# Mixture-of-experts block after a sketched attention: second expert product by seven half-width products on 2x2 blocks, token weights multiplied into x

## The chip, the cores and the metric

The kernel runs on one core of a Trainium2 chip. The metric is the device time of one execution in microseconds. A core has a matrix engine (PE, TensorE), a vector engine (DVE), a scalar engine (ACT), a general engine (POOL, GpSimd) and an engine that issues transfers (SP). Each engine works through its own list of instructions in order and waits on semaphores for the others. PE reads its operands from SBUF and writes to PSUM, which has eight banks of 512 float32 columns on 128 partitions.

## What is computed

The input of the second block is the output of the first, so both are in the kernel. All of it is float32.

```python
# attention: batch 4, heads 4, sequence 1088, head_dim 32, r = 8
def phi(x):                                   # 64 products of two sketches
    a = np.einsum('rd,bhsd->bhsr', S1, x)
    b = np.einsum('rd,bhsd->bhsr', S2, x)
    return np.einsum('bhsi,bhsj->bhsij', a, b).reshape(*x.shape[:-1], r * r)
q_p, k_p = (phi(q), phi(k))
kv = np.einsum('bhsf,bhsd->bhfd', k_p, v)
z = np.sum(k_p, axis=2)
num = np.einsum('bhsf,bhfd->bhsd', q_p, kv)
den = np.einsum('bhsf,bhf->bhs', q_p, z)[..., None] + 1e-06
x = num / den                                 # as 4352 tokens x 128
# routing and experts: N = 4352 tokens, D = 128, E = 8 experts, F = 1024
P = np.exp(x @ w_gate - (x @ w_gate).max())
for _ in range(8):
    P /= P.sum(1, keepdims=True) + 1e-09
    P /= P.sum(0, keepdims=True) + 1e-09
    P *= N / E
for e in range(E):
    h = np.maximum(x @ w1[e], 0.0)
    out += P[:, e:e + 1] * (h @ w2[e])
```

P is positive. A product with it may therefore stand in front of the maximum with zero as well as behind the second product.

## The kernel before

**Attention** (lines 184 to 255) runs four times, once for a batch of 1088 tokens. A pass transposes k and q on DVE (L187 to L191), projects k on PE (L197, L201), copies that to SBUF on ACT (L199, L202), forms the 64 products of the keys on DVE (L207), and sums them with v on PE (L214). DVE masks the sums (L221, L222). Then three chunks of 384, 352 and 352 tokens follow. A chunk projects q by four matmuls on two halves of PE's rows (L235), copies two of the four results on ACT (L238), multiplies them with the other two on DVE (L239), and forms denominators and numerators by four matmuls on two halves of PE's columns (L244). DVE adds a constant, takes a reciprocal and multiplies (L247 to L249), which gives the chunk's columns of `xT`, that is x with its 128 features on partitions. At the end of a pass come the logits: matmuls of 128 tokens each with `w_gate` as the moving operand of 8 columns (L254).

**Routing** (lines 263 to 298) is a chain on DVE with one small matmul on PE in each of its eight rounds (L285), for the sums over tokens. At its end the weights are spread over partitions (L296, L298).

**Experts** (lines 344 to 358): outside the 8 experts, inside 9 tiles of 512 tokens (the last has 256). A tile takes 8 blocks of 128 hidden units; each is one matmul of the first product (L351), a maximum with zero on ACT (L353), and one matmul of the second product one block later (L340), which accumulates in PSUM. DVE transposes the sum of a tile and expert in blocks of 32 (L324), multiplies it with the tokens' weights (L331) and adds it to `acc` (L332). The last expert's tiles are stored by SP (L311).

**What sets the order.** The kernel is written in the order attention, routing, experts, for a scheduler that sorts the instructions of each engine by the order in which they are written and by when their operands and buffers are to be had. The attention and the routing take their PSUM from a pool of four banks (`aps`, through `bank()`), the first product from a pool of two (`hps`), the second from another of two (`yps`). In the built program matmuls of expert 0 stand between those of the attention from the second pass on, and two pairs of them between each two rounds of the routing. The weights of expert 0 are loaded at the start from POOL's queue, the other experts' from the same queue, and k, q and v from SP's.

A matmul of float32 shows in the trace as two records, each with a weight load of its own.

Of the kernel before, what the change touches and what calls it, by code (L numbers as in the profile page):

```python
# [18 lines left out]
def f64_to_f32(nc, pool, raw, shape):  # L19
    """Pairs of 32-bit words (low, high) of float64 to float32, rounded to nearest: the upper 24 bits  # L20
    of the mantissa are a float32 by themselves, and the 29 bits below are added to it."""
# [15 lines left out]
    # The power of two, with its sign.  # L37
# [8 lines left out]
    # Below float32's normal range: zero; above it: infinite.  # L46
# [8 lines left out]
def kernel(  # L55
# [26 lines left out]
    UP = 2.0 ** 64  # L82

    consts = ctx.enter_context(tc.tile_pool(name="consts", bufs=1))
    big = ctx.enter_context(tc.tile_pool(name="big", bufs=1))
    ld = ctx.enter_context(tc.tile_pool(name="ld", bufs=2))
    wk = ctx.enter_context(tc.tile_pool(name="wk", bufs=2))
    wpool = ctx.enter_context(tc.tile_pool(name="wpool", bufs=3))
    hpool = ctx.enter_context(tc.tile_pool(name="hpool", bufs=4))
    ypool = ctx.enter_context(tc.tile_pool(name="ypool", bufs=3))  # L90
    sk = ctx.enter_context(tc.tile_pool(name="sk", bufs=2))
    hps = ctx.enter_context(tc.tile_pool(name="hps", bufs=2, space=PSUM))
    yps = ctx.enter_context(tc.tile_pool(name="yps", bufs=2, space=PSUM))
    aps = ctx.enter_context(tc.tile_pool(name="aps", bufs=4, space=PSUM))

    def bank():
        return aps.tile([P, 512], F32, tag="a", name="a")

# [8 lines left out]
    for i in range(2):  # L107
        t = consts.tile([P, H + 1, NT + 1, D], F32, name=f"v{i}")
        nc.gpsimd.memset(t[:, 2], 1.0)
        v_slots.append(t)  # L110
# [23 lines left out]
    weights = {}  # L134

    def load_w(e):
        w1 = wpool.tile([P, F], F32, tag="w1", name="w1")
        w2 = wpool.tile([P, FO, DM], F32, tag="w2", name="w2")
        nc.gpsimd.dma_start(out=w1, in_=moe_w1[e])  # L139
        nc.gpsimd.dma_start(out=w2, in_=moe_w2[e].rearrange("(fo fi) d -> fi fo d", fi=P))  # L140
        weights[e] = w1, w2
# [3 lines left out]
    load_w(0)  # L145

# [9 lines left out]
    rep = consts.tile([P, 4, 32], F32, name="rep")  # L156
    for c in range(4):
        sl = slice(32 * c, 32 * (c + 1))
        nc.gpsimd.tensor_copy(rep[sl], ident[sl, sl].unsqueeze(1).to_broadcast([32, 4, 32]))

    # The projections: wd gives a head's a and b, wq gives them repeated to the 64 products of a head.
# [15 lines left out]
    # Columns of x: (b, a, s).  # L177
    xT = big.tile([P, N], F32, name="xT")
    lg = big.tile([P, NG, E], F32, name="lg")
    acc = big.tile([P, NB, 32], F32, name="acc")  # L180
    prep = big.tile([P, NG, 4, E], F32, name="prep")

# [1 line left out]
    def attention(b):  # L184
# [8 lines left out]
        # Keys: a and b with tokens on partitions, their products, and the sums with v and 1.  # L193
# [22 lines left out]
        # Two heads together: the blocks of a head with the other's are zero.  # L216
# [10 lines left out]
        # Queries: the products with tokens in columns, then numerators and denominators.  # L227
# [22 lines left out]

        g0, g1 = b * S // P, (b + 1) * S // P
        pg = bank()[:, 0:(g1 - g0) * E].rearrange("p (g e) -> p g e", e=E)
        for g in range(g0, g1):
            nc.tensor.matmul(pg[:, g - g0, :], xT[:, P * g:P * (g + 1)], wg, start=True, stop=True)  # L254
        nc.scalar.copy(lg[:, g0:g1, :], pg)

    for b in range(B):
        attention(b)
        if b + 1 < 3:
            load_w(b + 1)  # L260

# [1 line left out]
    def routing():  # L263
        mx = sk.tile([P, 1], F32, tag="mx", name="mx")
        nc.vector.tensor_reduce(out=mx, in_=lg, axis=AX.XY, op=Alu.max)
        pm = bank()[:, 0:P]
        nc.tensor.matmul(pm, mx.to_broadcast([P, P]), ident, start=True, stop=True)
        nc.vector.reduce_max(mx, pm, axis=AX.X)
        nc.vector.tensor_scalar(mx, mx, -1.0, 64 * math.log(2.0), op0=Alu.mult, op1=Alu.add)
        pw = sk.tile([P, NG, E], F32, tag="p2", name="p2")  # L270
        nc.scalar.activation(out=pw, in_=lg, func=Act.Exp, bias=mx[:, 0:1])
        # float32's smallest step, 2^-149, which the exponentials are multiples of.
        step = 1.5 * 2.0 ** (23 - 149 + 64)
        nc.vector.tensor_scalar(pw, pw, step, step, op0=Alu.add, op1=Alu.subtract)
        for _ in range(ITERS):
            rs = sk.tile([P, NG], F32, tag="rs", name="rs")
            nc.vector.reduce_sum(rs, pw, axis=AX.X)
            nc.vector.tensor_scalar(rs, rs, 1.0 / UP, 1e-9, op0=Alu.mult, op1=Alu.add)
            nc.vector.reciprocal(rs, rs)
            p1 = sk.tile([P, NG, E], F32, tag="p1", name="p1")  # L280
            nc.vector.tensor_tensor(p1, pw, rs.unsqueeze(2).to_broadcast([P, NG, E]), op=Alu.mult)
            cs = sk.tile([P, E], F32, tag="cs", name="cs")
            nc.vector.reduce_sum(cs, p1.rearrange("p g e -> p e g"), axis=AX.X)
            pc = bank()[:, 0:E]
            nc.tensor.matmul(pc, ones, cs, start=True, stop=True)  # L285
            cr = sk.tile([P, E], F32, tag="cr", name="cr")
            nc.vector.tensor_scalar(cr, pc, 1.0 / UP, 1e-9, op0=Alu.mult, op1=Alu.add)
            nc.vector.reciprocal(cr, cr)
            pw = sk.tile([P, NG, E], F32, tag="p2", name="p2")
            nc.vector.scalar_tensor_tensor(pw, p1, float(N) / E, cr.unsqueeze(1).to_broadcast([P, NG, E]),  # L290
                                           op0=Alu.mult, op1=Alu.mult)
        # From partitions (c, s) to (any of four, s), as the outputs' blocks have them.
        for c in range(4):
            sl = slice(32 * c, 32 * (c + 1))
            pp = bank()[:, 0:NG * E]
            nc.tensor.matmul(pp, rep[sl].rearrange("p r s -> p (r s)"), pw[sl].rearrange("p g e -> p (g e)"),  # L296
                             start=True, stop=True, tile_position=(32 * c, 0))
            nc.scalar.mul(prep[:, :, c, :], pp.rearrange("p (g e) -> p g e", e=E), 1.0 / UP)  # L298

    routing()  # L300
    pcols = prep.rearrange("p g c e -> p (g c) e")

# [1 line left out]
    tiles = [(lo, min(lo + 512, N)) for lo in range(0, N, 512)]  # L304

    def store(b0, b1):
        while b0 < b1:
            b, a = divmod(b0, SA)
            m = min(b1 - b0, SA - a)
            for r in range(4):  # L310
# [3 lines left out]
                    in_=acc[32 * r:32 * (r + 1), b0:b0 + m, :])  # L314
            b0 += m

    def combine(e, lo, hi, yp):
        b0, b1 = lo // 32, hi // 32
        part = acc[:, b0:b1, :]
        if e == 0:  # L320
            nc.vector.transpose(out=part.rearrange("p b d -> p (b d)"), in_=yp)  # L321
            return
        yt = ypool.tile([P, 16, 32], F32, tag="yt", name="yt")[:, 0:b1 - b0, :]
        nc.vector.transpose(out=yt.rearrange("p b d -> p (b d)"), in_=yp)  # L324

        def weight(i):
            return pcols[:, b0:b1, i].unsqueeze(2).to_broadcast([P, b1 - b0, 32])

        if e == 1:
            nc.vector.tensor_tensor(part, part, weight(0), op=Alu.mult)  # L330
        nc.vector.tensor_tensor(yt, yt, weight(e), op=Alu.mult)  # L331
        nc.vector.tensor_tensor(part, part, yt, op=Alu.add)  # L332
        if e == E - 1:
            store(b0, b1)

    waiting = []

    def second():
        e, lo, hi, fo, hT, yp = waiting.pop(0)
        nc.tensor.matmul(yp, weights[e][1][:, fo, :], hT, start=(fo == 0), stop=(fo == FO - 1))  # L340
        if fo == FO - 1:
            combine(e, lo, hi, yp)

    for e in range(E):
        if e not in weights:
            load_w(e)
        for lo, hi in tiles:
            yp = yps.tile([P, 512], F32, tag="y", name="y")[:, 0:hi - lo]
            for fo in range(FO):
                hp = hps.tile([P, 512], F32, tag="h", name="h")[:, 0:hi - lo]  # L350
                nc.tensor.matmul(hp, weights[e][0][:, P * fo:P * (fo + 1)], xT[:, lo:hi], start=True, stop=True)  # L351
                hT = hpool.tile([P, 512], F32, tag="hT", name="hT")[:, 0:hi - lo]
                nc.scalar.activation(out=hT, in_=hp, func=Act.Relu)  # L353
                waiting.append((e, lo, hi, fo, hT, yp))
                if len(waiting) > 1:
                    second()
    while waiting:
        second()
# [30 lines left out]
```

## Time and profile before

| what | us |
|---|---|
| median of 3 runs | 1061.43 |
| lowest, highest | 1061.02, 1062.99 |
| span of the profiled execution, first to last instruction | 1058.4 |
| PE busy in that span | 1032.3 |
| ACT busy, DVE busy, POOL busy | 347.7, 240.8, 14.8 |
| L351 and L340, busy | 562.5 and 561.5 |
| last `xT` of the four attention passes written | 54.6, 83.3, 110.9, 135.9 |
| routing, from its first DVE instruction to its last on ACT | 138.7 to 174.9 |
| last matmul's start, end of the span | 1052.4, 1058.4 |

The profiled execution's span is 3.0 us shorter than the median of the runs, which count what lies around the span too. Busy times of matmuls overlap, since one's end is drawn behind the next one's start; what a matmul costs is read from the distance between starts. In the profile's clock row, and in the clock column of its tables, the first record is at 38.2 us; a full clock shown ahead of that is not a reading.

### The profile page before, as it was taken

What the parts mean: (1) busy time and instruction counts of PE and PEld (TensorE: products, weight loads), DVE (VectorE), ACT (ScalarE), POOL (GpSimd) and SP (SyncE); (2) the same over time, 40 slices, a digit from 0 to 9 for tenths busy, and PEclk for the clock granted to TensorE, in tenths of its full rate; (3) what the DMA queues carried; (4) which work ended last, traced back from release to release, by engine and by line L of the source; (5) the groups of instructions that cost most, each with busy time, mean ns of one, the idle gap of its engine ahead of it and who ended that gap; (6) DMA issues with size and microseconds to landing.
All of it is one profiled execution on the core that took longest, in us unless ns stands there. A gap on an engine that the chain in (4) does not pass through costs nothing.

```text
span 1058.4 us, 7579 instructions
## 1 busy us (share of the span) xinstructions
PE 1032.3 (98%) x2806; PEld 499.9 (47%) x2806; DVE 240.8 (23%) x405; ACT 347.7 (33%) x618; POOL 14.8 (1%) x34
## 2 busy tenths in 40 slices
PE   3999999999999999999999999999999999999997
PEld 3555544454444544454445444454445444454444
DVE  3665565111111211111111111111111111121112
ACT  0122223333333333333333333333333333333332
POOL 2000000000000000000000000000000000000000
PEclk9999999999999999999999999999999999999999
DMA  7200000000000100010000100010000000001111
GB/s 267 85 22 1 1 1 0 1 21 20 0 1 0 40 0 1 0 41 0 1 0 1 40 1 0 1 40 1 1 0 1 0 1 0 1 0 21 20 20 25
DMA packets 25683, 17.78 MB, mean 17 GB/s; under 512 B 20528, under 2 KB 22576, under 8 KB 25648
## 3 DMA queue, kind: packets, MB, share of 16 engines
q1 hardware_dynamic: 23168, 8.92, 3.2%
q0 software_dynamic: 2304, 8.39, 2.5%
q8 instruction: 22, 0.36, 0.1%
q14 instruction: 13, 0.11, 0.0%
q10 hardware_dynamic: 176, 0.01, 0.0%
HBM read 15.08 MB, written 2.23 MB: 16 GB/s over the span
## 4 chain that ended last, share of the span: by engine, by line
PE 96%; DMA 1%; DVE 1%; issue 0%; SPq 0%; ACT 0%; DVEq 0%; ACTq 0%
PE h L351 44%; PE y L340 44%; PE a L235 2%; PE a L244 2%; PE a L214 2%; DMA kx<-in_k_dram 1%; PE a L254 1%; DMA v<-in_v_dram 1%; PE a L197 1%; DVE kT L187 0%; DVE qa L239 0%; PE a L285 0%; SPq L123 0%; DVE kp L207 0%; PE a L201 0%
## 5 line engine op out<-in xcount | busy, mean ns | idle before, releaser
L351 PE MATMUL h<-xT,w 128*128 128x512 f32 (+1 forms) x1152 | 562.5, 570 | 0.0
L340 PE MATMUL y<-hT,w 128*128 128x512 f32 (+1 forms) x1152 | 561.5, 569 | 0.1
L353 ACT ACTIVATE hT<-h 128x512 f32<-128x512 f32 (+1 forms) x576 | 330.2, 573 | 610.5 <-PE h L351 610.5
L340 PEld LDWEIGHTS y<-hT,w 128*128 128x128 f32 x1152 | 217.4, 190 | 248.1 <-issue 236.5
L351 PEld LDWEIGHTS h<-xT,w 128*128 128x128 f32 x1152 | 217.5, 190 | 243.5 <-issue 240.1
L324 DVE STREAM_TRANSPOSE yt<-y 128x512 f32<-128x512 f32 (+1 forms) x63 | 43.3, 687 | 686.4 <-PE y L340 686.4
L331 DVE TENSOR_TENSOR yt<-yt,prep 128x512 f32<-128x512 f32 (+1 forms) x63 | 41.7, 662 | 2.1
L332 DVE TENSOR_TENSOR acc<-acc,yt 128x512 f32<-128x512 f32 (+1 forms) x63 | 41.7, 662 | 2.1
L238 ACT COPY qa<-a 128x352 f32<-128x352 f32 (+1 forms) x24 | 11.1, 461 | 61.9 <-PE a L235 61.9
L214 PE MATMUL a<-v,kp 128*128 128x96 f32 x144 | 23.9, 321 | 6.9 <-DVE kp L207 6.9
L235 PE MATMUL a<-qT,wq 64*128 64x352 f32 (+1 forms) x96 | 29.8, 546 | 0.0
L248 DVE RECIPROCAL rd<-rd 128x352 f32<-128x352 f32 (+1 forms) x12 | 29.0, 2416 | 0.4
L214 PEld LDWEIGHTS a<-v,kp 128*128 128x128 f32 x144 | 21.5, 225 | 11.0 <-DVE kp L207 7.0
L235 PEld LDWEIGHTS a<-qT,wq 64*128 64x128 f32 x96 | 14.4, 208 | 12.2 <-issue 6.1
L197 PE MATMUL a<-wd,kT 128*128 128x64 f32 x64 | 9.6, 313 | 10.8 <-DVE wd L171 10.8
L244 PE MATMUL a<-qa,kz 128*64 128x352 f32 (+1 forms) x48 | 15.8, 544 | 2.7 <-DVE qa L239 2.7
L321 DVE STREAM_TRANSPOSE acc<-y 128x512 f32<-128x512 f32 (+1 forms) x9 | 6.1, 679 | 53.7 <-PE y L340 53.7
L244 PE MATMUL a<-qa,kv 128*64 128x352 f32 (+1 forms) x48 | 15.5, 526 | 0.0
L197 PEld LDWEIGHTS a<-wd,kT 128*128 128x128 f32 x64 | 9.1, 227 | 10.7 <-issue 10.7
L139 POOL DMA_DIRECT2D w<-in_moe_w_dram x8 | 4.6, 578 | 682.6 <-PE h L351 682.6
L239 DVE TENSOR_TENSOR qa<-qa,a 128x352 f32<-128x352 f32 (+1 forms) x24 | 12.0, 509 | 5.2 <-PE a L235 4.9
L207 DVE TENSOR_TENSOR kp<-ab 128x1024 f32<-128x1024 f32 (+1 forms) x12 | 10.9, 946 | 3.8 <-ACT ab L199 3.8
(73 smaller groups left out, 118.2 us busy)
## 6 DMA issues: line engine op xcount, KB each, us to landing
w<-in_moe_w_dram POOLq DMA_DIRECT2D x16, 512.0 KB, 4.9
kx<-in_k_dram SPq DMA_DIRECT2D x4, 544.0 KB, 4.3
qx<-in_q_dram SPq DMA_DIRECT2D x4, 544.0 KB, 3.3
v<-in_v_dram SPq DMA_DIRECT2D x32, 64.0 KB, 2.0
out_dram<-acc SPq DMA_DIRECT2D x20, 64.0 KB, 1.9
v<-in_v_dram SPq DMA_DIRECT2D x16, 8.0 KB, 3.0
out_dram<-acc SPq DMA_DIRECT2D x4, 56.0 KB, 1.8
out_dram<-acc SPq DMA_DIRECT2D x4, 48.0 KB, 1.8
```

Source lines behind the costliest of these rows:

```text
L197: nc.tensor.matmul(pk[:, t].rearrange("p n f -> p (n f)"), kT[:, P * t:P * (t + 1)], wdf, start=True, stop=True)
L214: nc.tensor.matmul(pv[:, i], kp[0:n, g:g + 2].rearrange("p h i j -> p (h i j)"), vx[0:n, 2 * i:2 * i + 3, t, :], start=(t == 0), stop=(t = ...
L235: nc.tensor.matmul(t[:, 0:n], wqf[sl, m, :], qT[sl, lo:hi], start=True, stop=True, tile_position=(64 * i, 0))
L239: nc.vector.tensor_tensor(qa[:, 0:n], qa[:, 0:n], pb[:, 0:n], op=Alu.mult)
L244: nc.tensor.matmul(t[64 * i:64 * (i + 1), 0:n], w[:, i].rearrange("p h d -> p (h d)"), ph[i][:, 0:n], start=True, stop=True, tile_position ...
L248: nc.vector.reciprocal(rd[:, 0:n], rd[:, 0:n])
L324: nc.vector.transpose(out=yt.rearrange("p b d -> p (b d)"), in_=yp)
L331: nc.vector.tensor_tensor(yt, yt, weight(e), op=Alu.mult)
L332: nc.vector.tensor_tensor(part, part, yt, op=Alu.add)
L340: nc.tensor.matmul(yp, weights[e][1][:, fo, :], hT, start=(fo == 0), stop=(fo == FO - 1))
L351: nc.tensor.matmul(hp, weights[e][0][:, P * fo:P * (fo + 1)], xT[:, lo:hi], start=True, stop=True)
L353: nc.scalar.activation(out=hT, in_=hp, func=Act.Relu)
```

## The change

The second product is done on 2x2 blocks. Two tiles of tokens (t = 0, 1) and two neighbouring blocks of hidden units (f = 0, 1) make the four blocks h0 to h3; `w2` is split into two halves of 64 output columns. Where the plain way takes eight products of 64 output columns, seven are formed here, from sums of blocks: the sums of `w2` come from POOL (`ws`, four additions for each load of an expert), the sums of h from DVE (`ts`, four subtractions for each four blocks of h). The seven go to four accumulators in PSUM, and their sums are taken apart once for each group (`evacuate`).

Both products are now made of matmuls of 64 output columns, which stand alternately on the left and on the right half of PE's columns (`tile_position` 0 and 64). The built program has 1,280 of them in the first product and 1,120 in the second.

The loops are exchanged: outside 5 pairs of token tiles (three of 2x448, two of 2x416), inside the experts. A step of four h blocks and seven products is a quad; there are 160. Expert 0 goes first over three pairs without weights, and is weighted when it is added; elsewhere the weights multiply x on POOL (`xe`), from a copy of P that goes through DRAM (`pT`) and back to all partitions (`pb`). Each expert is loaded anew for each pair, by SP.

The logits are made at the end of each chunk, with `w_gate` (8 columns) as the weights and the chunk's `xT` as the moving operand, and land transposed (`lgT`). The first product uses the pool `aps` (through `bank()`) that attention and routing use; `hps` and `yps` are gone, and four banks hold the accumulators.

In the built program PE's list is: attention passes 1 to 4, in each of them the chunk's logits ahead of the next chunk's L235; then all nine matmuls of the routing; then the experts. No matmul of an expert stands ahead of the routing's last.

Cut to its core:

```diff
-    hps = ctx.enter_context(tc.tile_pool(name="hps", bufs=2, space=PSUM))
-    yps = ctx.enter_context(tc.tile_pool(name="yps", bufs=2, space=PSUM))
     aps = ctx.enter_context(tc.tile_pool(name="aps", bufs=4, space=PSUM))
+    mps = ctx.enter_context(tc.tile_pool(name="mps", bufs=1, space=PSUM))
+    dram = ctx.enter_context(tc.tile_pool(name="dram", bufs=1, space=bass.MemoryType.DRAM))
...
+    def load_w(e, queue):
         w1 = wpool.tile([P, F], F32, tag="w1", name="w1")
         w2 = wpool.tile([P, FO, DM], F32, tag="w2", name="w2")
-        nc.gpsimd.dma_start(out=w1, in_=moe_w1[e])
-        nc.gpsimd.dma_start(out=w2, in_=moe_w2[e].rearrange("(fo fi) d -> fi fo d", fi=P))
-        weights[e] = w1, w2
+        queue.dma_start(out=w1, in_=moe_w1[e])
+        queue.dma_start(out=w2, in_=moe_w2[e].rearrange("(fo fi) d -> fi fo d", fi=P))
+        ws = wpool.tile([P, 4, FO // 2, H2], F32, tag="ws", name="ws")
+        a11, a21 = w2[:, 0::2, 0:H2], w2[:, 0::2, H2:DM]
+        a12, a22 = w2[:, 1::2, 0:H2], w2[:, 1::2, H2:DM]
+        nc.gpsimd.tensor_tensor(ws[:, 0], a21, a22, op=Alu.add)
+        nc.gpsimd.tensor_tensor(ws[:, 1], ws[:, 0], a11, op=Alu.subtract)
+        nc.gpsimd.tensor_tensor(ws[:, 2], a11, a21, op=Alu.subtract)
+        nc.gpsimd.tensor_tensor(ws[:, 3], a12, ws[:, 1], op=Alu.subtract)
+        return w1, w2, ws
...
-        g0, g1 = b * S // P, (b + 1) * S // P
-        pg = bank()[:, 0:(g1 - g0) * E].rearrange("p (g e) -> p g e", e=E)
-        for g in range(g0, g1):
-            nc.tensor.matmul(pg[:, g - g0, :], xT[:, P * g:P * (g + 1)], wg, start=True, stop=True)
-        nc.scalar.copy(lg[:, g0:g1, :], pg)
+            pg = bank()[32 * b:32 * b + E, 0:n]
+            nc.tensor.matmul(pg, wg, xT[:, b * S + lo:b * S + hi], start=True, stop=True,
+                             tile_position=(0, 32 * b))
+            nc.scalar.copy(lgT[32 * b:32 * b + E].rearrange("p a s -> p (a s)")[:, lo:hi], pg)
...
+        nc.vector.transpose(out=lgp.rearrange("p a e -> p (a e)"), in_=lgT.rearrange("p a s -> p (a s)"))
+        lg = lgp[:, :, 0:E]
...
+        nc.vector.transpose(out=lgT.rearrange("p a s -> p (a s)"), in_=lgp.rearrange("p a e -> p (a e)"))
+        for b in range(B):
+            nc.sync.dma_start(out=pT[:, b * S:(b + 1) * S],
+                              in_=lgT[32 * b:32 * b + E].rearrange("p a s -> p (a s)"))
...
+    groups = [(i, [0], False) for i in range(PLAIN)]
+    groups += [(i, list(range(1 if i < PLAIN else 0, E)), True) for i in range(NP)]
+    items = [(g, e) for g, (_, es, _) in enumerate(groups) for e in es]
...
+        pb = late.tile([P, 2 * NMAX], F32, tag="pb", name="pb")[:, 0:2 * n]
+        nc.sync.dma_start(out=pb, in_=pT[e:e + 1, lo:lo + 2 * n].to_broadcast([P, 2 * n]))
+        xe = late.tile([P, 2 * NMAX], F32, tag="xe", name="xe")[:, 0:2 * n]
+        nc.gpsimd.tensor_tensor(xe, xT[:, lo:lo + 2 * n], pb, op=Alu.mult)
+        sources[j] = xe
...
+    def evacuate(g):
+        i, _, weighted = groups[g]
+        lo, n = pair(i)
+        m = []
+        for k in range(4):
+            t = late.tile([P, NMAX], F32, tag=f"m{k}", name="m", bufs=1)[:, 0:n]
+            if k % 2:
+                nc.vector.tensor_copy(t, sums[g][k])
+            else:
+                nc.scalar.copy(t, sums[g][k])
+            m.append(t)
...
+    def first(k, c):
+        j, q = quads[k]
+        n = pair(groups[items[j][0]][0])[1]
+        if c == 0:
+            hs[k] = (hpool.tile([P, 4, NMAX], F32, tag="h", name="h")[:, :, 0:n],
+                     hpool.tile([P, 4, NMAX], F32, tag="t", name="t", bufs=3)[:, :, 0:n])
+        f, t = 2 * q + c // 2, c % 2
+        ph = bank()[:, 0:n]
+        order = (0, 1) if k % 2 == 0 else (1, 0)
+        for s in order:
+            sl = slice(H2 * s, H2 * (s + 1))
+            nc.tensor.matmul(ph[sl], loaded_w[j][0][:, P * f + H2 * s:P * f + H2 * (s + 1)],
+                             sources[j][:, t * n:(t + 1) * n], start=True, stop=True,
+                             tile_position=(0, H2 * s))
+        h, ts = hs[k]
+        nc.scalar.activation(out=h[:, c], in_=ph, func=Act.Relu)
+        if c == 3:
+            nc.vector.tensor_tensor(ts[:, 0], h[:, 1], h[:, 0], op=Alu.subtract)
+            nc.vector.tensor_tensor(ts[:, 1], h[:, 3], h[:, 1], op=Alu.subtract)
+            nc.vector.tensor_tensor(ts[:, 2], h[:, 3], ts[:, 0], op=Alu.subtract)
+            nc.vector.tensor_tensor(ts[:, 3], ts[:, 2], h[:, 2], op=Alu.subtract)
...
+        p1 = (w2[:, 2 * q, lo], h[:, 0], 0, 0)
+        p6 = (ws[:, 1, q], ts[:, 2], 0, 1)
+        p2 = (w2[:, 2 * q + 1, lo], h[:, 2], 1, 0)
+        p4 = (w2[:, 2 * q + 1, hi], ts[:, 3], 1, 1)
+        p3 = (ws[:, 3, q], h[:, 3], 2, 0)
+        p5 = (ws[:, 0, q], ts[:, 0], 2, 1)
+        p7 = (ws[:, 2, q], ts[:, 1], 3, k % 2)
+        if k % 2 == 0:
+            return [p1, p6, p2, p4, p3, p5, p7]
+        return [p6, p1, p4, p2, p5, p3, p7]
...
+        nc.tensor.matmul(sums[g][i][H2 * s:H2 * (s + 1)], w, x, start=is_first, stop=is_last,
+                         tile_position=(0, H2 * s))
+    for k in range(len(quads) + LAG):
+        if k < len(quads) and quads[k][1] == 0:
+            j = quads[k][0]
+            if j == 0:
+                prepare(0)
+            if j + 1 < len(items):
+                prepare(j + 1)
+        todo = products(k - LAG) if k >= LAG else []
+        for c in range(4):
+            if k < len(quads):
+                first(k, c)
+            for p in todo[2 * c:2 * c + 2]:
+                second(k - LAG, p)
```

## The prediction

> **What bounds the kernel now.** I read the page's busy shares first, then its slices and costliest groups.
>
> ```profile
> span 1058.4 us, 7579 instructions
> ...
> PE 1032.3 (98%) x2806; PEld 499.9 (47%) x2806; DVE 240.8 (23%) x405; ACT 347.7 (33%) x618; POOL 14.8 (1%) x34
> ...
> PE   3999999999999999999999999999999999999997
> ...
> L351 PE MATMUL h<-xT,w 128*128 128x512 f32 (+1 forms) x1152 | 562.5, 570 | 0.0
> L340 PE MATMUL y<-hT,w 128*128 128x512 f32 (+1 forms) x1152 | 561.5, 569 | 0.1
> ```
>
> PE is busy from the second slice to the end, in the attention (to 135.9 us) and the routing (to 174.9) too, because the experts' matmuls fill the holes there. So matmul time is the bound, and a hole costs its length. A record of 512 columns starts 0.429 us after the one before it (160.507, 160.936), one of 256 columns after 0.2155. Experts before: 2048 x 0.429 + 256 x 0.2155 = 933.8 us. From 174.9 to the last matmul at 1052.8 are 877.9 us; the other 56 us were done beside attention and routing.
>
> The next view is PE's timeline, at one matmul group in two states of the clock (start, duration, instruction):
>
> ```profile
> 10.77 3.65 PE L197 MATMUL a<-wd,kT 128*128 128x64 f32 x16 [10.77 <-DVE wd L171]
> ```
>
> ```profile
> 50.32 1.98 PE L197 MATMUL a<-wd,kT 128*128 128x64 f32 x16
> ```
>
> The same 16 records take 3.65 us early and 1.98 us later: PE begins at half its clock. The table by stretches (PE's busy time second, the clock third from the right) shows what opens and shuts it:
>
> ```profile
> 31.40:34.80 3.40, 2.79 (x9) 1.30 (x8) 1.68 (x3) 0.96 (x2) 0.00 (x0) 1.00 0.58 181
> 34.80:38.20 3.40, 3.40 (x11) 1.70 (x8) 2.15 (x3) 0.00 (x0) 0.00 (x0) 1.00 0.95 362
> 38.20:41.60 3.40, 1.92 (x7) 0.67 (x5) 3.40 (x5) 0.90 (x2) 0.00 (x0) 1.00 0.00 0
> 41.60:45.00 3.40, 3.40 (x10) 1.35 (x10) 1.92 (x5) 0.00 (x0) 0.00 (x0) 0.50 0.01 2
> ```
>
> Matmul durations are halved-clock ones through the first two rows (records 0.64 us apart for 384 columns). Busy 2.79 of 3.4 us did not open the clock, 3.40 of streaming did (full from 38.2), 1.92 of 3.4 shut it again (0.50), 3.40 opened it. From 45 us on it stays full, with PE never idle.
>
> **The experts: gain.** Whether two 64-column matmuls run side by side is read from L244, which has them on both halves of the columns:
>
> ```profile
> 47.70 0.46 PE L244 MATMUL a<-qa,kv 128*64 128x352 f32 x1
> 47.85 0.51 PE L244 MATMUL a<-qa,kz 128*64 128x352 f32 x1
> 48.00 0.46 PE L244 MATMUL a<-qa,kv 128*64 128x352 f32 x1
> 48.20 0.46 PE L244 MATMUL a<-qa,kz 128*64 128x352 f32 x1
> ```
>
> On one half (kv) the records are 0.296 us apart, what 352 columns need, while the other half (kz) runs between them: the halves are independent. With 0.429 us for 512, a record of 448 takes 0.376 and one of 416 0.349. A quad is 15 half-width matmuls of two records, on two halves at once: 15 x 0.376 = 5.64 us, or 5.24. 96 x 5.64 + 64 x 5.24 = 876.8 us. Gain: 57.0 us.
>
> What lies beside it: four ACT maxima in a quad (0.60 us at 512 columns and 0.38 at 256, so 0.54 each) make 2.2 us; four DVE subtractions at L332's 0.692 and 0.425 (0.63 each) make 2.5 us: both under 5.64, no new bound. The four accumulators of a group finish one after another, and each is copied (0.5 us) a quad before its next use: nothing. POOL does four additions of 256 and one of 896 elements in an item's 22 us. No row has them; between L159's 0.29 us and four of L207's (1.21 for 1024), 1 to 6 us, so nothing. Loads, 1 MB of weights and 0.46 MB of `pb` in 22 us, are 66 GB/s, where the first slice moved 267. If one of these covers failed, an item would be late by its excess.
>
> The Trainium skill ("TensorE: Matmul & The Clock Gate", Measured speedup vs the span model) gives 2.38 times for three column tiles, not 3. Taken over to two halves (1.59) it would make 1753 / 1.59 = 1103 us of the experts, an estimate; the row above shows two streams at full rate, and decides.
>
> **The attention: loss.** In the built program PE's list has no expert's matmul ahead of the routing's end, and the logits of a chunk stand in front of the next chunk's L235. PE takes its list in order, so from a chunk's reciprocal to its `xT` nothing can run on PE, and the next chunk begins only then. Before, a chunk took 5.7 us, L235 lying beside the reciprocal:
>
> ```profile
> 43.65 0.53 DVE L247 TENSOR_SCALAR rd<-a 128x352 f32<-128x352 f32 x1 [1.45 <-PE a L244]
> 44.21 2.35 DVE L248 RECIPROCAL rd<-rd 128x352 f32<-128x352 f32 x1
> 46.48 0.46 DVE L239 TENSOR_TENSOR qa<-qa,a 128x352 f32<-128x352 f32 x1
> 46.86 0.51 DVE L249 TENSOR_TENSOR xT<-a,rd 128x352 f32<-128x352 f32 x1
> ```
>
> A chunk now, from `xT` to `xT`, at half clock: logits 0.1 + 1.17 (352 columns, two records of 0.587), 0.14 to the next group, L235 2.35 (four matmuls on two row halves), 0.34 until DVE, L239 0.46, L244 0.06 + 2.35 + 0.37, then 0.53 + 2.35 + 0.51 and 0.1 between them: 10.8 us. At full clock the same chain is 7.6. At half clock PE streams for 3.66 us (1.17 of it on 8 columns), pauses 0.9, streams 2.9 and idles 3.3; at full clock it streams 45% of the time, with the same idle end. By the four rows a stretch seldom falls so that it opens the clock, and the idle end shuts it again, so I take half clock.
>
> The first chunk of a pass, half clock: logits 1.27; 0.14; L197 and L201 3.69 to ACT (10.77 to 14.46); copy 0.59; L207 to L214 1.25; L214 8.72 (21.68 to 30.40) with one L235 put in between, 1.56; then L235's other three, L239 and L244, 5.5, and 3.7 of DVE: 26.4 us. At full clock 17.2. A pass is 26.4 + 21.6 = 48.0 us, or 32.4 at full clock; before, 28.7 and 27.6, with 7 us of experts' matmuls in each.
>
> The first pass: L207 began at 20.4, behind a load of k that landed at 19.2 beside three experts' weights (3.1 MB). Only one expert is loaded there now. But the memsets for `wd` and `wq` now stand on POOL's list behind three `ws` additions, which wait for `w2` (landed at 9.1); DVE's L171 started at 9.92 and now waits for them. With 0.3 to 1.2 us for an addition L207 starts between 16.3 and 18.5; I take 17.4. To its first `xT`: 26.4 - 5.7, and 1.1 for a transpose of k that DVE does ahead of it (37.11): 39.2. Two chunks: 60.8. Three passes: 204.8.
>
> **The routing: loss.** It used to be covered whole. Logits' copy 2.1 us, one transpose of 1088 columns 1.31 (L191), 3.25 to the first round (138.70 to 141.95), seven rounds of 3.66 (146.09 to 149.75, with no wait for PE), 2.7 up to the eighth's matmul: 35.0. Experts start at 239.8.
>
> **Ramp, end and sum.** PE begins the experts at half clock, and a clock that opens after one to two stretches of 3.4 us costs half of those, 2.6 us. End: before, 6.0 us from the last matmul. Now a copy 0.53, a copy on ACT 0.5, four DVE steps of 0.58, a transpose of 0.58, eight store issues of 0.48 that cover the second transpose (before: four), 0.4 of handing on, and 2.4 to the end as before: 10.5. Two stretches of full clock in the attention, -2.6. 239.8 + 2.6 + 876.8 + 10.5 - 2.6 = 1127.1; with the 3.0 around the span, **1130**. Against before: experts' matmuls -57.0; the 56 us done under attention and routing now begin only at 239.8 instead of 174.9, which with ramp and end outweighs it by 69.
>
> **Rivals.** *The clock stays full in the attention.* First pass 54.4, passes 32.4 each, routing 34.6: experts start at 186.2, the time is 1079. For it: from 48.4 to 51.8 us short matmuls (L254, L197) kept the clock. Against it: the third row. The skill (same page, Part 1) says that the clock falls after an idle window of about 3.4 us and advises no gap over that; the chunk's gap is 3.3, so by that rule it would stay. The rows shut it after a gap of 1.5 us (39.8 to 41.3). The rule alone would make 1079, the rows 1130.
>
> *The halves get in each other's way.* The first record of a group takes 0.346 instead of 0.296 (47.85 to 48.20). If each of 1,200 matmuls on a half pays 0.05, 60 us: 1190. If the halves ran one after the other, 1753 us: about 2000. Against both: the steady 0.296.
>
> *Faster.* The attention, freed of the experts' matmuls, is bound by PE's own work alone. Less its 17 and 16 experts' records (0.43 each) a pass was 21 us. Then the experts start at 39.2 + 11.4 + 3 x 21 + 34.6 = 148, and the time is 1041. The sign turns at a start of 168.5 (1058.4 - 876.8 - 2.6 - 10.5). Against it: it needs L235 to pass the waiting logits.
>
> **Chances.** Half clock, 1110 to 1148: 0.64 (forecast 1130). Clock full for a good part, 1079 to 1110: 0.18. Halves in each other's way, 1150 and up: 0.12, half of that to 1190. Faster or same: 0.06, of which 0.01 within 0.2%, which is about what a measurement of this kernel can tell from no change. The range from 1085 to 1165 takes in the first, most of the second and some of the third, and the bounds of POOL's additions (1 us each way) and of L207's start.
>
> **What would show it.** Right: PE nearly empty between its groups in the first nine slices, L197's 16 records at 3.65 us in passes 2 to 4, no experts' matmul before about 235 us, then PE at 9 in each slice with a quad of 5.64 us. Wrong: L197 at 1.98 us (the clock rival); quads of 6 us or more (the halves); experts before 170 us. An ACT or DVE wait in front of the second product would show a cover that failed.

## The result and the profile after

The changed kernel takes 1124.99 us (median; 1121.92 to 1130.92), the kernel before 1061.22 us (1060.30 to 1062.99). The ratio is 1.0609, with a 95% interval of 1.0578 to 1.0641: slower by 6.1%. The forecast was 1130.

The lines of the page of the kernel after that answer to those shown of before: span, busy shares, PE's slices, the granted clock in the same slices, and the costliest groups.

```profile
span 1123.4 us, 13161 instructions
...
PE 1012.3 (90%) x5250; PEld 424.9 (38%) x5250; DVE 596.1 (53%) x934; ACT 387.5 (34%) x734; POOL 214.3 (19%) x206
...
PE   4675775189999999999999999999999999999996
...
PEclk9758668589999999999999999999999999999998
...
L423 PE MATMUL a<-xe,w 128*64 128x448 f32 (+1 forms) x2368 | 684.4, 527 | 0.0
...
L462 PE MATMUL s<-t,ws 128*64 128x448 f32 (+1 forms) x960 | 415.0, 528 | 1.6 <-DVE t L432 1.6
```

PE was 98% busy and is 90% busy. The hole is in the first eight slices of 28.1 us, the attention and the routing; the experts begin in the ninth (digit 8), and from the tenth on PE is full, at full clock. The table by stretches (us; PE busy, PEld, DVE, ACT, POOL, clock, DMA share, GB/s) puts numbers to it: the first row is the fourth pass of the attention, the second the routing, the third the experts, the fourth the end.

```profile
150.40:194.70 44.30, 31.37 (x108) 18.60 (x108) 16.85 (x22) 4.82 (x11) 0.00 (x0) 0.69 0.00 1
194.70:229.80 35.10, 6.18 (x22) 4.65 (x22) 24.65 (x66) 0.96 (x2) 0.00 (x0) 0.52 0.00 0
229.80:1112.10 882.30, 879.80 (x4801) 344.75 (x4800) 484.15 (x729) 365.10 (x686) 201.17 (x177) 1.00 0.21 65
1112.10:1123.40 11.30, 0.14 (x1) 0.00 (x0) 5.15 (x10) 1.35 (x3) 0.00 (x0) 0.60 0.25 38
```

The experts have no hole: 879.8 us busy in 882.3. They take 933.8 - 882.3 = 51.5 us less than before, but they begin at 229.8; before, 56 of their 933.8 us were already done at 174.9. What PE waits for, in the view of waits (us in total, times, longest):

```profile
PE a L257 <- DVE xT L255: 36.8, 11, 3.6
PE a L290 <- DVE cs L288: 26.4, 8, 3.8
PE a L203 <- DVE wd L175: 14.0, 1, 14.0
```

The first line is the logits' wait for a chunk's `xT`, the second the routing's rounds. The kernel before had neither among its waits, since experts' matmuls lay there. Its whole list:

```profile
PE a L197 <- DVE wd L171: 10.8, 1, 10.8
PE a L214 <- DVE kp L207: 6.9, 1, 6.9
PE a L244 <- DVE qa L239: 2.7, 4, 1.5
```

### The profile page after: what moved, and what is told of

Same layout as the page of the kernel before. It is cut to its first block, busy times and chain, and to the rows that moved or that the text cites. A ratio compares the mean times of both kernels' runs of the same rounds, so it can differ in the third digit from the quotient of the medians.

```text
span 1123.4 us, 13161 instructions
## 1 busy us (share of the span) xinstructions
PE 1012.3 (90%) x5250; PEld 424.9 (38%) x5250; DVE 596.1 (53%) x934; ACT 387.5 (34%) x734; POOL 214.3 (19%) x206
## 4 chain that ended last, share of the span: by engine, by line
PE 86%; DVE 10%; DMA 1%; issue 1%; ACT 0%; POOL 0%; DVEq 0%; POOLq 0%
PE a L423 40%; PE s L462 35%; PE a L241 3%; PE a L220 3%; DVE rd L254 3%; PE a L250 2%; PE a L203 1%; PE a L257 1%; DMA w<-in_moe_w_dram 1%; DMA pb<-pT 1%; DVE xT L255 1%; DVE rd L253 1%; DVE cs L288 0%; PE a L290 0%; DVE qa L245 0%
## 5 line engine op out<-in xcount | busy, mean ns | idle before, releaser
L423 PE MATMUL a<-xe,w 128*64 128x448 f32 (+1 forms) x2368 | 684.4, 527 | 0.0
L427 ACT ACTIVATE h<-a 128x448 f32<-128x448 f32 (+1 forms) x640 | 341.5, 534 | 539.2 <-PE a L423 532.7
L462 PE MATMUL s<-t,ws 128*64 128x448 f32 (+1 forms) x960 | 415.0, 528 | 1.6 <-DVE t L432 1.6
L423 PEld LDWEIGHTS a<-xe,w 128*64 128x64 f32 x2368 | 246.4, 137 | 260.1 <-issue 258.8
L431 DVE TENSOR_TENSOR t<-h 128x448 f32<-128x448 f32 (+1 forms) x160 | 142.4, 890 | 306.2 <-ACT h L427 306.2
L462 PE MATMUL s<-h,w 128*64 128x448 f32 (+1 forms) x640 | 285.6, 528 | 0.0
L462 PEld LDWEIGHTS s<-t,ws 128*64 128x64 f32 x960 | 131.2, 137 | 137.8 <-issue 133.8
L462 PE MATMUL s<-t,w 128*64 128x448 f32 (+1 forms) x320 | 143.1, 529 | 0.9 <-DVE t L433 0.9
L430 DVE TENSOR_TENSOR t<-h 128x448 f32<-128x448 f32 (+1 forms) x160 | 101.3, 633 | 80.2 <-ACT h L427 80.2
L462 PE MATMUL s<-h,ws 128*64 128x448 f32 (+1 forms) x320 | 142.9, 528 | 0.0
L432 DVE TENSOR_TENSOR t<-h,t 128x448 f32<-128x448 f32 (+1 forms) x160 | 101.8, 636 | 0.0
L462 PEld LDWEIGHTS s<-t,w 128*64 128x64 f32 x320 | 43.7, 137 | 51.8 <-issue 46.1
L257 PE MATMUL a<-xT,wg 128*8 128x352 f32 (+1 forms) x24 | 11.8, 578 | 42.0 <-DVE xT L255 36.8
L241 PE MATMUL a<-qT,wq 64*128 64x352 f32 (+1 forms) x96 | 38.1, 805 | 0.0
```

The lines of the kernel that those rows point to most:

```text
L241: nc.tensor.matmul(t[:, 0:n], wqf[sl, m, :], qT[sl, lo:hi], start=True, stop=True, tile_position=(64 * i, 0))
L423: nc.tensor.matmul(ph[sl], loaded_w[j][0][:, P * f + H2 * s:P * f + H2 * (s + 1)], sources[j][:, t * n:(t + 1) * n], start=True, stop=True ...
L427: nc.scalar.activation(out=h[:, c], in_=ph, func=Act.Relu)
L430: nc.vector.tensor_tensor(ts[:, 0], h[:, 1], h[:, 0], op=Alu.subtract)
L431: nc.vector.tensor_tensor(ts[:, 1], h[:, 3], h[:, 1], op=Alu.subtract)
L432: nc.vector.tensor_tensor(ts[:, 2], h[:, 3], ts[:, 0], op=Alu.subtract)
```

## The experiments

**Theory.** The experts gain about what was worked out. The loss is one of order: the pool shared by attention and first product keeps the experts' matmuls behind the routing; the logits, at the end of each chunk, hold the next chunk on PE; and a PE that idles runs at half clock. **Rival.** The half-width products, the sums on POOL and DVE or the weighted x cost time by themselves.

The table gives all of it (times in us; the ratio to the kernel before on the same chip, with its interval). "Last `xT`" is the end of the attention; "experts start" is their first matmul.

| kernel | last `xT` | experts start | last matmul starts | span | ratio |
|---|---|---|---|---|---|
| before | 135.9 | under the attention | 1052.4 | 1058.4 | 1 |
| before_one_pool | 156.5 | 192.6 | 1128.8 | 1134.8 | 1.0698 (1.0682 to 1.0714) |
| after | 194.7 | 229.8 | 1111.7 | 1123.4 | 1.0609 (1.0578 to 1.0641) |
| fill | 172.9 | 208.0 | 1090.7 | 1102.3 | 1.0395 (1.0378 to 1.0413) |
| logits_last | 156.9 | 192.1 | 1074.4 | 1086.0 | 1.0225 (1.0207 to 1.0243) |
| two_pools | 206.0 | 56.6 | 1088.0 | 1099.7 | 1.0367 (1.0351 to 1.0382) |
| two_pools_last | 171.9 | 51.8 | 1052.4 | 1064.0 | 1.0063 (1.0039 to 1.0087) |
| eight | 200.6 | 236.0 | 1173.5 | 1180.9 | 1.1102 (1.1077 to 1.1128) |
| mixed | 141.6 | 49.0 | 1007.6 | 1020.3 | 0.9606 (0.9591 to 0.9621) |

**One pool in the kernel before.** The kernel before, with nothing changed but the pool of the first product's PSUM:

```diff
-    hps = ctx.enter_context(tc.tile_pool(name="hps", bufs=2, space=PSUM))
-                hp = hps.tile([P, 512], F32, tag="h", name="h")[:, 0:hi - lo]
+                hp = bank()[:, 0:hi - lo]
```

> The kernel before, with one edit: the first product takes its PSUM from the pool of four banks that attention and routing use, and its own pool of two is gone. Nothing else of the change is in it. Theory (the pool decides the order, and the lost cover is the price): no expert's matmul before the routing's end, experts start at about 205 us (passes of 37 to 40 us, routing 35), then 934 us of experts: 1140 to 1160 us. Rival (the order comes from the exchanged loops or the 2x2 products, and the pool does nothing): 1055 to 1070 us.

Measured: 1135.53 us. Its page (busy in slices, clock) and its first wait:

```profile
PE   3899953999999999999999999999999999999997
...
PEclk9966675999999999999999999999999999999999
```

```profile
PE a L284 <- DVE cs L282: 26.5, 8, 3.8
```

The same picture as after the change: an uncovered routing with 26.5 us of waits, and a clock at half in it. No expert's matmul stands before the routing's end. So the shared pool alone sets the order, with old products, old logits, old loops. It costs 76.4 us of span: the experts' free run starts 17.7 us later (192.6 for 174.9) and has 58.6 us more to do. The time is a little below the expected 1140 to 1160, because the passes are shorter than was taken: 34.4, 34.1 and 31.6 us for 37 to 40. From here to the kernel after: 37.2 us of later start, 54.2 us less in the experts (936.1 to 881.9 from their first matmul to the last one's start), 5.7 us more at the end, together 11.4 less. The rest of the change is a gain already with this loss in it.

**Logits at the end of the pass.** The three logits matmuls of a pass behind its third chunk, each with its own bounds; nothing else.

```diff
+        for lo, hi in ((0, 384), (384, 736), (736, S)):
-            pg = bank()[32 * b:32 * b + E, 0:n]
+            pg = bank()[32 * b:32 * b + E, 0:hi - lo]
```

> The changed kernel, with the three logits matmuls of a pass written behind its third chunk instead of each behind its own chunk. Theory (a chunk's logits hold the next chunk's L241 behind the xT): the step from xT to xT in a pass falls from 8 to 11 us to 6 to 7.5, less two more logits matmuls at the end of a pass: passes of 39 to 42 us instead of 44, total 1105 to 1118 us. Rival (the chunks are bound by the chain on DVE, the place of the logits is harmless): 1120 to 1130 us.

Measured: 1085.15 us, 39.8 less than after: the theory's sign, but two to six times its size (7 to 20 us were expected, and a step of 6 to 7.5 us). One chunk of the kernel after, from the chain of waits (start, duration, what):

```profile
88.01 0.57 DVE xT L255
...
88.71 0.81 PE a L257 x2
89.52 1.48 PE a L241 x8
...
91.58 1.45 PE a L250 x6
...
93.61 2.36 DVE rd L254
...
96.07 0.54 DVE xT L255
```

And of this run, DVE's and PE's timelines (start, duration):

```profile
78.97 2.35 DVE L254 RECIPROCAL rd<-rd 128x352 f32<-128x352 f32 x1
81.24 0.46 DVE L245 TENSOR_TENSOR qa<-qa,a 128x352 f32<-128x352 f32 x1
81.61 0.51 DVE L255 TENSOR_TENSOR xT<-a,rd 128x352 f32<-128x352 f32 x1
```

```profile
78.89 2.25 PE L241 MATMUL a<-qT,wq 64*128 64x352 f32 x8
```

After the change, L241 begins when the last chunk's `xT` and its logits are done: 8.0 us from `xT` to `xT`, at full clock. In this run L241 of the next chunk lies beside the reciprocal of this one, and the step is 5.1 us. The step is 3 us shorter at an equal clock, and most steps of the kernel after ran partly at half clock besides. With 11.2 us in the first pass and 26.6 in the three others, this is the attention's 37.8 (194.7 to 156.9). The attention now ends where it did with one pool in the kernel before (156.5), and the experts start at 192.1 for 192.6. So the loss falls into three parts: 76.4 us for the pool, 37.7 for the place of the logits and 5.7 at the end, against 54.2 gained in the experts; that makes 65.6, and the two spans lie 65.0 apart.

**Filling the holes.** The logits stay at the chunk's end; five matmuls into a spare bank, whose results nobody reads, run while DVE takes the reciprocal.

```diff
+    spare = mps.tile([P, 512], F32, tag="s0", name="spare")
...
+            for _ in range(5):
+                nc.tensor.matmul(spare[:, 0:n], ident, ph[1][:, 0:n], start=True, stop=True)
```

> The changed kernel, with five matmuls of 352 or 384 columns added behind the L250 of each chunk, into a bank that the attention does not use; their results are not read. They only keep PE busy while DVE takes the reciprocal. Theory (half clock costs about 12 us a pass): L203's 16 records at 2.0 us instead of 3.65, passes of 33 to 37 us instead of 44, total 1085 to 1100 us, although PE has 60 matmuls more. Rival (the clock is not what makes the passes long): the added 2.9 us or more of each chunk stand in front of the logits, no gain, 1125 to 1160 us.

Measured: 1103.82 us, a little over the expected stretch; the passes of 38.8, 39.4 and 37.8 us are so too (33 to 37 were expected). Its table by stretches, passes 2 and 4:

```profile
56.90:95.70 38.80, 34.32 (x138) 20.92 (x138) 19.16 (x25) 4.81 (x11) 0.00 (x0) 0.87 0.05 15
...
135.10:172.90 37.80, 34.16 (x138) 20.76 (x138) 16.85 (x23) 4.82 (x11) 0.00 (x0) 0.86 0.00 1
```

30 more records in a pass, and the pass is 4.7 to 6.5 us shorter: the clock is 0.83 to 0.87 for 0.69 to 0.73, and the second and third chunk take 8.0 us each. L203, which is L205 in this run, begins each of these passes at full clock, as expected:

```profile
57.71 2.00 PE L205 MATMUL a<-wd,kT 128*128 128x64 f32 x16
```

But the clock falls a few us later (in pass 2 it is at 0.50 from 63.3 to 73.5), after a stretch in which DVE transposes k and forms the products of the keys and PE has 0.92 us of work in 3.41. What the fillers open of the clock is worth 21.8 us (229.8 to 208.0 in the experts' start); what it still loses there is not in that figure. The other part of the chunk's loss is the order of PE's list, which a full clock does not mend.

**Two pools.** The kernel after with its four attention banks parted: two for attention and routing, two for the first product.

```diff
-    aps = ctx.enter_context(tc.tile_pool(name="aps", bufs=4, space=PSUM))
+    aps = ctx.enter_context(tc.tile_pool(name="aps", bufs=2, space=PSUM))
+    hps = ctx.enter_context(tc.tile_pool(name="hps", bufs=2, space=PSUM))
-        ph = bank()[:, 0:n]
+        ph = hps.tile([P, 512], F32, tag="h", name="ph")[:, 0:n]
```

> The changed kernel, with the four banks of the shared pool parted: two for attention and routing, two for the first product. Theory (the lost cover is the loss): experts' matmuls stand again between those of the second pass and later ones, the clock stays full from about 50 us, and the three unweighted groups (67 us) are done by the routing's end; some waits stay where the first group's copies need memory that the attention still holds, and some 10 us until the first weighted x is there: 1015 to 1050 us, below both kernels. Rival (two banks are too few for the attention, its chunks wait for PSUM): passes of 45 us or more and 1060 to 1100 us.

Measured: 1100.46 us. The theory's number was wrong, and the rival's right to its edge. Experts' matmuls did move under the attention (the first at 56.6 us), but passes took 46.5, 42.5 and 50.7 us, and the last of them held none (108 records, clock 0.56). Its waits:

```profile
PE a L258 <- DVE xT L256: 20.4, 8, 3.9
...
PE ph L424 <- POOL xe L348: 11.0, 1, 11.0
```

The rival blamed the two banks. The first line still names the logits. So one more run tells the two apart:

**Two pools, logits at the end of the pass.** The run above, with the edit of the logits.

> The run with two banks for attention and two of its own for the first product (1100.5 us), with the three logits of a pass behind its third chunk. Theory (it is the place of the logits, which hold the chunk behind them on xT, that makes its passes 46 us even with full-clock matmuls of experts between): passes of 30 to 38 us, 1060 to 1085 in all. Rival (two banks are too few for the attention's chain, wherever the logits stand): passes stay at 43 us or more, and the time within 10 us of 1100.

Measured: 1070.06 us (1061.87 to 1073.31; its profiled execution took 1065.78). Passes of 39.6, 38.2 and 37.0 us, the wait on `xT` gone from the list. The theory's time held, and its passes nearly (30 to 38 were expected): it was again the logits' place that cost most, 30 us of the time. The two banks cost little: L242's waits until ACT and DVE have read a bank (`qa`) are 4.7 us in all. What keeps this kernel from being faster than the one before is mostly in these two waits, 26.3 us:

```profile
PE a L292 <- DVE cs L290: 15.9, 6, 7.9
...
PE ph L425 <- POOL xe L349: 10.4, 1, 10.4
```

Only 12 quads of expert 0 can go ahead of the routing's probabilities, 12 x 5.64 = 67.7 us. They are used up by 211 us; then the last rounds of the routing and the first weighted x stand open, at half clock from 215.0, to 237.4.

**Eight products instead of seven.** The kernel after; the sums of weights and of h are formed as before, but not used, and the two output tiles of a pair are simply copied out.

```diff
-        p1 = (w2[:, 2 * q, lo], h[:, 0], 0, 0)
-        p6 = (ws[:, 1, q], ts[:, 2], 0, 1)
...
+        for f in (0, 1):
+            for t in (0, 1):
+                pair_ = [(w2[:, 2 * q + f, H2 * s:H2 * (s + 1)], h[:, 2 * f + t], t, s, f) for s in (0, 1)]
+                out += pair_ if k % 2 == 0 else pair_[::-1]
```

> The changed kernel with the second product of a 2x2 block as eight plain half-width products in place of seven; the seven products' sums and differences of weights and of h are still computed, but not used, so that VectorE and GpSimd do the same work, and the two output tiles of a pair are evacuated by a plain copy. Theory (a quad is bound by the number of half-width records, two of which go through in 0.376 us): one more of 15 halves per quad, 882.3/15 = 58.8 us more in the experts, 1175 to 1190 in all. Rival (the quad is bound by something else than the count of halves, by relu, by the sums of h or by weight loads): less than 50 us more, under 1170.

Measured: 1178.61 us, 53.6 more than with seven. The experts' row:

```profile
236.00:1173.90 937.90, 937.90 (x5121) 359.95 (x5121) 472.41 (x671) 345.57 (x648) 189.33 (x177) 1.00 0.20 61
```

The experts are 55.6 us longer (937.9 for 882.3), the attention 5.9, and the end 4.3 shorter (7.0 for 11.3), since nothing is taken apart there. A quad of 16 halves is worth 16/15 of one of 15: 876.8 x 16/15 = 935.3, and half of the 6.0 us that the clock took to open (242.1) makes 938.3, for 937.9 measured. So a quad is bound by its number of records, and the seven products in place of eight are worth what they were priced at. The attention's 5.9 us are no part of that: its matmuls are the same in both kernels, but the clock was 0.57 to 0.66 in passes 2 to 4 here and 0.69 to 0.73 there. So much did its opening differ between two executions of the same work.

**Mixed.** Order and products put together: expert 0 goes the plain way of the kernel before, with two banks for each product, as cover under attention and routing; its banks are closed, and experts 1 to 7 follow by seven products over five pairs. The logits stand at the end of the pass.

```diff
+    aps = early_ps.enter_context(tc.tile_pool(name="aps", bufs=4, space=PSUM))
+    hps = early_ps.enter_context(tc.tile_pool(name="hps", bufs=2, space=PSUM))
+    yps = early_ps.enter_context(tc.tile_pool(name="yps", bufs=2, space=PSUM))
...
+            nc.tensor.matmul(hp, first_w[0][:, P * fo:P * (fo + 1)], xT[:, lo:lo + n], start=True, stop=True)
...
+    early_ps.close()
+    mps = ctx.enter_context(tc.tile_pool(name="mps", bufs=1, space=PSUM))
+    fps = ctx.enter_context(tc.tile_pool(name="fps", bufs=4, space=PSUM))
-    groups = [(i, [0], False) for i in range(PLAIN)]
-    groups += [(i, list(range(1 if i < PLAIN else 0, E)), True) for i in range(NP)]
+    groups = [(i, list(range(1, E)), True) for i in range(NP)]
```

> Expert 0 goes the plain way of the kernel before (full-width matmuls, two banks for the first product and two for the second, attention and routing on the other four), so that its 116.7 us of matmul can lie under attention and routing; its banks are then closed, and experts 1 to 7 go by seven half-width products with weighted x, in five pairs of token tiles. The logits of a pass stand behind its third chunk. Theory (the change lost its time by the order of attention, routing and experts alone; the seven products and the weighted x are worth what the records say): against the kernel before, seven of the eight experts gain 57.0 x 7/8 = 50 us of matmul, the end takes 5.3 us more and the rest stays: 1061.2 - 50 + 5.5 = 1017 us, 1010 to 1025. Rival (the changing over of the PSUM banks, or the first weighted x, which needs routing's probabilities and then a product on GpSimd, leaves a hole of 10 us or more, or the cover under attention is thinner than in the kernel before): 1025 to 1050.

Measured: 1020.18 us, ratio 0.9606 (0.9591 to 0.9621): faster than both kernels, by 3.9% and by 9.3% (1020.18 / 1124.99 = 0.907). Its page:

```profile
span 1020.3 us, 12523 instructions
...
PE 983.4 (96%) x4970; PEld 434.4 (43%) x4970; DVE 551.4 (54%) x845; ACT 377.4 (37%) x716; POOL 202.6 (20%) x192
...
PE   3999999999999999999999999999999999999995
...
PEclk9999999999999999999999999999999999999998
```

PE is full from the second slice on, as in the kernel before, with 49 us less of busy time (983.4 for 1032.3). No pool's turnover and no weighted x leaves a hole (0.8 us is the one wait there). Its passes are 33.4, 28.1 and 29.3 us. From the last matmul's start the end takes 12.7 us, 6.7 more than before, where 5.3 was expected.

## Why the prediction was right, point by point

**The mechanism held.** Experts behind the routing, chunk behind chunk, a clock shut in between, and a steady PE afterwards: each was named and each is in the trace. The run with one pool shows that the first comes from the pool, the run with the logits moved that the second comes from their place, the run with the fillers that the third costs by itself. The sign named for the clock, L203's 16 records at 3.65 us in passes 2 to 4, came whole in pass 2 and in part in passes 3 and 4 (3.17 and 3.13 us):

```profile
63.61 3.68 PE L203 MATMUL a<-wd,kT 128*128 128x64 f32 x16
```

The time was 5.0 us under the forecast, 3.7 of it in the span and the rest in what lies around it (1.6 us for 3.0); by terms (us):

| term | forecast | measured |
|---|---|---|
| end of the first pass | 60.8 | 62.5 |
| passes 2 to 4 | 48.0 each | 43.5, 44.4, 44.3 |
| credit for two stretches of full clock | -2.6 | in the passes |
| routing | 35.0 | 35.1 |
| experts start | 239.8 | 229.8 |
| clock's opening and experts | 2.6 + 876.8 | 882.3 |
| from the last matmul to the end | 10.5 | 11.3 |
| span | 1127.1 | 1123.4 |

**The term that was mis-sized is the pass**, by 3 x 48.0 - 132.2 = 11.8 us in all (9.2 with the credit of 2.6), because the clock was taken as shut nearly everywhere. The first chunk of a pass was about right, 26.0, 25.4 and 25.4 us for 26.4; the miss is in the second and third chunks, 55.4 us for 64.8 in the three passes. I had read from before that 1.92 us of streaming in a stretch of 3.4 shuts the clock and that 2.79 does not open it. In pass 2 (the table by stretches, PE busy second, the granted clock third from the right):

```profile
80.20:83.60 3.40, 3.40 (x10) 1.61 (x11) 1.73 (x6) 0.48 (x1) 0.00 (x0) 0.51 0.29 82
83.60:87.00 3.40, 1.52 (x8) 0.61 (x6) 2.21 (x2) 0.00 (x0) 0.00 (x0) 1.00 0.00 0
87.00:90.40 3.40, 1.69 (x8) 0.91 (x10) 1.46 (x2) 0.53 (x2) 0.00 (x0) 1.00 0.00 0
90.40:93.80 3.40, 2.38 (x12) 0.90 (x8) 1.69 (x4) 0.84 (x2) 0.00 (x0) 1.00 0.00 0
93.80:97.20 3.40, 0.46 (x2) 0.12 (x2) 2.69 (x2) 0.00 (x0) 0.00 (x0) 1.00 0.00 0
97.20:100.60 3.40, 3.11 (x9) 1.21 (x8) 0.19 (x1) 1.12 (x3) 0.00 (x0) 0.50 0.00 0
```

Stretches with 1.52, 1.69 and 2.38 us busy kept the clock open; only the one with 0.46 shut it, and 3.11 opened it again (full from 100.6). So the clock was 0.69 to 0.73 in passes 2 to 4, not 0.5, and the chunks took 8.0 to 9.6 us there in place of 10.8 (in the first pass, 11.1 and 10.5, which is the forecast's chunk). At full clock a chunk took 8.0 us where 7.6 had been worked out; halving only what PE streams in the sum of 10.8 (1.17, 2.35 and 2.35) gives 7.9. Part of the miss is chance: the same passes took 140.2 us in the run with eight products. The Trainium skill ("TensorE: Matmul & The Clock Gate", Part 1: The HAM clock gate) lets the clock fall after an idle window of about 3.4 us, and these rows agree with that better than my reading did. Its advice to keep gaps under that was not enough here, though: the gap before 96.74 was 3.31 us, just under it, and the clock fell; in the kernel before it fell with 1.92 us busy and a gap of 1.5. Why 1.92 shut it there and 1.52 did not here stays open.

**The first pass** was 1.7 us late: L213 began at 18.3 instead of 17.4, and DVE took two transposes (1.30 and 1.19 us) in front of the first chunk's last steps, where one was counted.

**The routing** matched by luck: its rounds took 3.81 us, for 3.66 in the row they were taken from, and the steps around them less than put down.

**The experts.** The two halves run side by side at full rate. PE's timeline (start, duration):

```profile
500.19 0.54 PE L423 MATMUL a<-xe,w 128*64 128x448 f32 x1
500.20 0.54 PE L462 MATMUL s<-h,w 128*64 128x448 f32 x1
500.56 0.54 PE L462 MATMUL s<-t,w 128*64 128x448 f32 x1
500.57 0.54 PE L423 MATMUL a<-xe,w 128*64 128x448 f32 x1
```

Two records, one on each half, every 0.376 us: the figure forecast, twice the rate of one half. The 1.59 that had been estimated for two halves from three column tiles in the Trainium skill (the page named above, Measured speedup vs the span model) is not what these rows show. The 2.9 us over the forecast are nearly all three waits on DVE's sums of h, 2.5 us together; I had said that DVE sets no new bound, which holds for a quad on average, but not for each of them (the last section shows what held DVE). POOL's four additions for an expert take about 1.0 us each and the weighted x 2.07, about 6 us in an item, the upper bound; no wait of the changed kernel's experts names POOL.

**The rivals.** The halves are not in each other's way: the rows above show it, and the run with eight products, where a quad grew by its records. The clock that stays full would have given 1079; the run with fillers, where it is open for the larger part, gave 1104, because its chunks take 8.0 us for 7.6, and the first chunk of a pass 21.8 to 23.4 for 17.2, with the clock shut in the middle of it. That L241 would have to pass the waiting logits for a better time is what the run with the logits moved shows, at 1085; but its passes are 34 to 36 us, not the 21 of the rival that made the change faster.

**What I missed**, in the expectations: the logits' place was priced at 7 to 20 us and cost 40, and of the two pools alone I expected a gain. In both I had counted what a waiting logits matmul takes on PE, and not all that it holds behind it.

## What to carry to other kernels

Before a saving on the busiest engine is counted, look which work covers the serial phases, and whether the change still lets it (its buffers, and the data that it needs): here 54 us saved were outweighed by a lost cover (76 us) and by logits that held up the attention (38 us). A small matmul that waits for the end of another engine's chain holds all that stands behind it; put it where its operand is long there. Gain and cover need not exclude each other: seven experts kept the gain here, with the eighth as the old cover.

## What the runs showed of the hardware that was not expected

DVE's subtraction L431 takes 890 ns on average in the kernel after, its neighbour L430 of the same shape 633. The timelines of DVE and POOL show why:

```profile
498.35 2.04 DVE L431 TENSOR_TENSOR t<-h 128x448 f32<-128x448 f32 x1 [2.38 <-ACT h L427]
500.32 0.61 DVE L432 TENSOR_TENSOR t<-h,t 128x448 f32<-128x448 f32 x1
```

```profile
497.82 2.09 POOL L347 TENSOR_TENSOR xe<-xT,pb 128x896 f32<-128x896 f32 x1 [5.73 <-PE a L423]
```

A subtraction on DVE that meets POOL's product lasts until 0.5 us after it. 38 of the 640 lie mostly beside such a product and take 1.92 us on average; the 527 that meet no two-input work of POOL take 0.61. That is 50 us of DVE time in a run, and little of the span, since DVE is busy for about half of it. But the three waits of PE on DVE's sums have much to do with it. Each comes where a group's sums are taken apart, which is 5 us of work for DVE, and each stands behind a DVE instruction with two inputs that was drawn out beside POOL's product by more than PE then waited: to 1.97, 1.65 and 2.33 us from about 0.6, for waits of 0.2, 0.7 and 1.6. No run takes the product away to prove it. The longest was this one:

```profile
791.20 2.33 DVE L432 TENSOR_TENSOR t<-h,t 128x416 f32<-128x416 f32 x1
```

```profile
790.69 2.40 POOL L347 TENSOR_TENSOR xe<-xT,pb 128x832 f32<-128x832 f32 x1 [4.45 <-PE a L423]
```

The Trainium skill ("SBUF — State Buffer", Who interferes with whom) says that a DVE instruction with two inputs in SBUF and a GpSimd instruction that reads SBUF lock each other out for a whole instruction; these rows agree. Whoever moves a product to POOL should count it on DVE too.
